# A fused attention and squared-ReLU kernel: values of two groups in one TensorE visit, two half-size visits joined, and a new rule table

## The chip, the core and the metric

The kernel runs on one core of one Trainium2 chip. The metric is the device time of one execution in microseconds (us), lower is better. The core has a matrix engine (TensorE, PE in the profile, with its weight loads listed apart as PEld), VectorE (DVE), ScalarE (ACT), GpSimd (POOL), and SyncE (SP), which here only issues DMAs. Matmuls read SBUF and write PSUM; each engine works off its own instruction list in a fixed order and waits on semaphores for the others.

## What is computed

Two stages run one behind the other, over B = 4 batches of N = 12480 rows of C = 128 columns:

```
h   = mab(I, x)                  # 32 inducing rows attend to all 12480 rows of the batch
y   = mab(x, h)                  # every row of the batch attends to the 32 rows of h
mab(q, kv) = softmax(q @ kv.T / sqrt(128)) @ kv
out = (s * relu(y @ w_in)**2 + b) @ w_out       # d_ff = 2048
```

All data are float32. The first attention needs the whole batch before its softmax is known; the second attention and the two matrix products need only a block of rows and h.

## The kernel before

**Tiling.** A batch is cut into 26 blocks of 480 rows, so there are 104 blocks. For a block the products of the second stage are done in 8 *pairs* of 128 columns of d_ff, 832 pairs in all. A pair (function `pair`) is 8 matmuls of 128x128 weights and 480 columns: two form h (line 1002); `square` and `pair` take the ReLU's square apart into a rounded part and a remainder, and six matmuls into the output bank x (line 1112) take the rounded part with w_lo and w_hi and the remainder with w_hi. The remainder is made by one of three ways: a product on DVE and a subtraction on POOL (line 1056 on POOL, "way P"), both on DVE ("way D"), or a product on DVE and an accumulating DMA that POOL issues (line 1032, "way M").

**Front work.** Beside the pairs of a block runs one *front chain* (`front_work`) in the PSUM bank that the block's output doesn't use. It belongs to attention: for the next batch the scores against the inducing rows (`scores`, 7 groups: six of four blocks and one of two), their maximum (`top`), the values (`values`, 7 groups), the normalisation (`points`) and the small weight product (`w_tiles`); for this batch the second attention (`attend`, also six groups of four blocks and one of two). A block's output matmuls may not start before the front chain of the block ahead is done. The tables ATTEND_AT, SCORES_AT, VALUES_AT and so on say at which block of the batch each unit runs; loads are issued on SP two blocks earlier (AHEAD).

A scores or attention visit of TensorE is up to four matmuls of 128x32 weights and 480 columns, each into its own strip of 32 PSUM partitions. A values visit is 15 matmuls of 128x32 weights (the transposed exponentials, tile eT, three buffers) and 128 columns, which go round the four strips and accumulate; after each visit DVE adds the PSUM sums to the tile accb (line 813). The rows of x for it come in two tiles called xn, of which there are two buffers, so one group's tiles fill both.

**Order.** The program is not ordered by hand: `Plan.run` walks a model of the engines and picks the next instruction by urgency. The numbers of a `Rules` row are the urgencies and leanings it uses (which engine takes a ReLU, when way P, D or M is taken). OPENING holds for the first 16 pairs; then each row of STEADY holds for 32 pairs, four blocks.

Of the kernel before, what the change touches and what calls it, by code (L numbers as in the profile page):

```python
# [10 lines left out]
F32 = mybir.dt.float32  # L11
# [8 lines left out]
P = 128  # L20
# [65 lines left out]
class Rules:  # L86
# [15 lines left out]
    Rules(0.0201, 0.001, -0.4875, 0.022, -8.4567, 5.0037, 2.0571, -1.4711, -15.4208, 3.0931, 2.7863, -1.9358, 2.4132, 1, 0),  # L102
    Rules(0.0217, 0.001, -0.4875, 0.022, -8.4567, 5.0037, 2.0571, -1.4711, -15.4208, 3.0931, 2.0666, -1.9358, 2.4132, 1, 0),
    Rules(0.0167, 0.0365, -0.4924, -0.0196, -12.8895, 5.57, 3.612, -1.5635, -15.4208, 2.9768, 3.1193, 0.5521, 2.3739, 1, 0),
    Rules(0.015, 0.0134, -0.7399, -0.0848, -9.5023, 6.316, 2.0571, -1.5635, -17.0341, 3.1304, 2.2195, -1.3212, 2.9975, 1, 0),
    Rules(0.015, 0.0107, -0.8152, 0.022, -14.1641, 4.9158, -1.107, -0.559, -16.2261, 2.1922, 1.2773, -1.8274, 2.0319, 1, 0),
    Rules(0.0201, 0.0096, -0.624, -0.0242, -8.7384, 5.5129, 2.0571, -1.5635, -15.4208, 2.8109, 2.047, -1.5184, 2.5131, 1, 1),
    Rules(0.0163, 0.001, -1.0478, 0.0978, -8.4567, 8.7374, 2.6103, -1.6884, -17.2651, 3.9096, 3.0379, -2.4315, 2.8881, 1, 0),
    Rules(0.0166, 0.001, -0.624, -0.1167, -5.3436, 5.4916, 3.1805, -0.7229, -17.4773, 2.8109, 2.7209, -1.9358, 2.4761, 1, 0),
    Rules(0.0169, 0.0945, -0.5274, -0.0581, -9.2351, 5.0037, 2.6517, -1.5635, -15.4208, 3.8819, 2.6915, -1.145, 3.3157, 1, 0),  # L110
    Rules(0.015, 0.001, -0.4331, -0.0012, -11.1416, 1.583, -1.107, -0.682, -19.3219, 2.1922, 2.4768, -1.9358, 2.4367, 1, 0),
    Rules(0.0147, 0.001, -0.7361, 0.0372, -5.5428, 6.1406, -1.107, -1.2971, -16.2261, 2.1922, 2.6919, -2.4036, 1.9805, 1, 0),
    Rules(0.0133, 0.001, -0.7846, 0.0725, -10.853, 5.7978, -0.2013, -1.2971, -15.8209, 2.1922, 2.4641, -2.4036, 2.2634, 1, 0),
    Rules(0.0166, 0.084, -0.7108, 0.095, -5.3877, 5.0037, 2.7203, -1.5635, -15.8029, 1.6703, 2.6102, -2.1339, 2.3802, 1, 0),
    Rules(0.0166, 0.084, -0.624, -0.0484, -4.5286, 4.6079, 2.8543, -1.4194, -16.3935, 2.2965, 2.7381, -2.0738, 2.7526, 1, 1),
    Rules(0.0151, 0.084, -0.5751, 0.0036, -9.5767, 5.0037, 2.6127, -1.1092, -15.4208, 2.8842, 3.0781, -0.352, 3.2141, 1, 0),
    Rules(0.0151, 0.084, -0.5751, 0.0036, -9.5767, 5.0037, 2.6127, -1.1092, -15.4208, 2.8842, 3.0781, -0.352, 3.2141, 1, 0),
    Rules(0.0166, 0.084, -0.624, -0.0581, -9.3974, 5.588, 1.858, -1.5635, -15.4208, 3.8843, 1.1082, -0.9457, 2.9743, 1, 0),
    Rules(0.0188, 0.0593, -0.6897, -0.0335, -8.4567, 5.588, 2.6127, -1.9229, -13.1823, 2.6468, 2.5331, -2.1339, 1.9527, 1, 0),
    Rules(0.0199, 0.0017, -0.4795, -0.0514, -9.4081, 6.0969, 2.1224, -1.5635, -17.1933, 2.6161, 2.3942, -1.0923, 2.078, 1, 0),  # L120
# [126 lines left out]
def tile_attn_relu2(ctx: ExitStack, tc: tile.TileContext, xT, xN, xF, indT, w_in, w_out, s_rep, b_rep, outT):  # L247
# [132 lines left out]
    def load_early(j):  # L380
# [7 lines left out]
        plan.events["x", 0, j, 1] = landing(1.2)  # L388

    def load_xn(gate, b, g, half):  # L390
        n, free = ring_in_order("xn", 2)
        yield "SP", 0.05, *free, *gate
        rows = M * blocks_in(g)
        t = xn_pool.tile([P, TH, P], F32, name="xn")
# [934 lines left out]
```

## Time and profile before

| | |
|---|---|
| median of 3 runs | 1519.55 us (1518.22 to 1521.71) |
| the profiled execution | 1518.01 us, of which the span from first to last instruction is 1516.2 us |
| TensorE clock granted | 0.999 of full |
| matmul busy | 1495.3 us, 99% of the span |
| weight loads busy | 1294.9 us, 85% |
| DVE, ACT, POOL busy | 1435.3 us (95%), 1465.4 us (97%), 1443.7 us (95%) |

All engines are busy nearly all the time. A busy share is an average over stages. Matmul records overlap (a record of 0.37 us is followed by the next start 0.20 us later), so the price of a matmul is read from start to start.

### The profile page before, as it was taken

The numbers are of one execution on the slowest core, as the hardware profiler recorded it, in microseconds if no ns is written. First come the engines' busy times: TensorE is split into PE (matmuls) and PEld (weight loads), VectorE is DVE, ScalarE is ACT, GpSimd is POOL, SyncE is SP. The second block draws the span as 40 slices with busy tenths as digits, with TensorE's granted clock in tenths as the row PEclk, the third lists the DMA queues.
The fourth block names the chain that finished last, engine by engine and source line by source line (L and its number), as shares of the span: only waits on it lengthen the run. The fifth ranks groups of instructions, "written<-read, shape, count | busy, mean of one in ns | idle before, by whom it ended". The sixth has DMA issues, their size and how long they took to land.

```text
span 1516.2 us, 25236 instructions
## 1 busy us (share of the span) xinstructions
PE 1495.3 (99%) x8215; PEld 1294.9 (85%) x8215; DVE 1435.3 (95%) x1587; ACT 1465.4 (97%) x1767; POOL 1443.7 (95%) x725
## 2 busy tenths in 40 slices
PE   7899999999999999999999999999999999999998
PEld 5588888888888888888898888888889888888887
DVE  5899999999999999999999999999999999999998
ACT  6899999999999999999999999999999999999997
POOL 2599999999999999999999999999999999999998
PEclk9999999999999999999999999999999999999999
DMA  9244545534454454453455534544533334234332
GB/s 342 65 124 128 140 104 158 143 76 125 104 150 127 114 149 105 135 142 83 127 133 137 144 104 118 163 112 105 120 102 93 79 91 112 56 85 108 91 72 53
DMA packets 73810, 178.91 MB, mean 118 GB/s; under 512 B 13520, under 2 KB 40144, under 8 KB 73680
## 3 DMA queue, kind: packets, MB, share of 16 engines
q1 hardware_dynamic: 59280, 128.51, 27.2%
q0 software_dynamic: 14256, 48.67, 17.3%
q8 instruction: 67, 1.10, 0.3%
q14 instruction: 63, 0.52, 0.1%
q10 hardware_dynamic: 144, 0.12, 0.0%
HBM read 74.56 MB, written 25.56 MB: 66 GB/s over the span
## 4 chain that ended last, share of the span: by engine, by line
PE 69%; ACT 4%; issue 3%; POOL 3%; DVE 2%; DVEq 0%; ACTq 0%; POOLq 0%
PE x L1112 48%; PE h L1002 17%; POOL g L1056 3%; ACT r L1014 2%; ACT g L1080 2%; PE x L853 1%; DVE g L1045 1%; PE x L802 1%; PE x L762 1%; DVE h L1045 0%; DVE r L1016 0%; DVE gm L1027 0%; PE x L717 0%; ACT ob L1125 0%; POOL hm L1032 0%
## 5 line engine op out<-in xcount | busy, mean ns | idle before, releaser
L1056 POOL TENSOR_TENSOR g<-g,g 128x960 fp32r<-128x960 f32 x611 | 1399.2, 2665 | 21.7 <-DVE g L1045 13.4
L1112 PE MATMUL x<-g,w_hi 128*128 128x480 f32 x2932 | 920.1, 367 | 1.5 <-POOL g L1056 1.0
L1080 ACT ACTIVATE g<-r 128x960 fp32r<-128x960 f32 x733 | 713.4, 1008 | 12.0 <-PE x L1112 0.9
L1045 DVE SCALAR_TENSOR_TENSOR g<-h,r 128x960 f32<-128x960 f32 x611 | 688.5, 1146 | 24.2 <-ACT r L1014 13.7
L1014 ACT ACTIVATE r<-h 128x960 f32<-128x960 f32 x648 | 608.6, 970 | 12.5 <-PE h L1002 10.2
L1112 PEld LDWEIGHTS x<-g,w_hi 128*128 128x128 f32 x2932 | 550.8, 189 | 52.5 <-issue 6.3
L1112 PE MATMUL x<-g,w_lo 128*128 128x480 f32 x1466 | 537.4, 367 | 1.4 <-ACT g L1080 1.1
L1002 PE MATMUL h<-a2t,wst 128*128 128x480 f32 x1664 | 485.4, 374 | 3.7 <-DVE g L1045 3.2
L1002 PEld LDWEIGHTS h<-a2t,wst 128*128 128x128 f32 x1664 | 299.2, 189 | 82.2 <-issue 33.1
L1112 PEld LDWEIGHTS x<-g,w_lo 128*128 128x128 f32 x1466 | 277.0, 189 | 24.5 <-issue 2.6
L1016 DVE TENSOR_SCALAR r<-h 128x960 f32<-128x960 f32 x184 | 210.8, 1148 | 5.0 <-PE h L1002 3.8
L1056 DVE TENSOR_TENSOR g<-h,g 128x960 fp32r<-128x960 f32 x122 | 140.7, 1153 | 7.8 <-ACT g L1080 1.2
L1045 DVE SCALAR_TENSOR_TENSOR h<-h,r 128x960 f32<-128x960 f32 x122 | 141.0, 1155 | 0.9 <-ACT r L1014 0.8
L1027 DVE SCALAR_TENSOR_TENSOR gm<-h,r 128x960 f32<-128x960 f32 x99 | 113.3, 1145 | 4.3 <-ACT r L1014 4.1
L1032 POOL DMA_DIRECT2D hm<-gm x99 | 113.7, 1148 | 0.1
L1080 ACT ACTIVATE hm<-r 128x960 fp32r<-128x960 f32 x99 | 99.7, 1007 | 0.7
L1112 PE MATMUL x<-hm,w_lo 128*128 128x480 f32 x198 | 72.8, 368 | 0.0
L1112 PE MATMUL x<-hm,w_hi 128*128 128x480 f32 x198 | 72.5, 366 | 0.0
L1125 ACT ACTIVATE ob<-x,bias 128x480 f32<-128x480 f32 x101 | 66.8, 661 | 1.1 <-PE x L1112 0.5
L1112 PE MATMUL x<-hm,w_neg 128*128 128x480 f32 x198 | 56.3, 366 | 0.0
L1112 PEld LDWEIGHTS x<-hm,w_lo 128*128 128x128 f32 x198 | 37.4, 189 | 3.5 <-DVE hl L891 0.8
L1112 PEld LDWEIGHTS x<-hm,w_neg 128*128 128x128 f32 x198 | 37.4, 189 | 2.7
(152 smaller groups left out, 559.4 us busy)
## 6 DMA issues: line engine op xcount, KB each, us to landing
hm<-gm POOLq DMA_DIRECT2D x99, 480.0 KB, 5.3
xt<-in_xT_dram SPq DMA_DIRECT2D x96, 480.0 KB, 5.2
a2t<-hl SPq DMA_DIRECT2D x412, 60.0 KB, 2.0
out_dram<-ob SPq DMA_DIRECT2D x103, 240.0 KB, 2.1
xn<-in_xN_dram SPq DMA_DIRECT2D x18, 512.0 KB, 4.3
xn<-in_xN_dram SPq DMA_DIRECT2D x18, 448.0 KB, 4.8
wst<-whl SPq DMA_DIRECT2D x48, 64.0 KB, 2.0
g<-in_w_in_dram SPq DMA_DIRECT2D x4, 512.0 KB, 10.3
```

The lines of the kernel that those rows point to most:

```text
L762: nc.tensor.matmul(ps[M * q:M * (q + 1), 0:BLK], ind_sb, xt[:, q % SB], start=True, stop=True)
L802: nc.tensor.matmul(ps[M * c:M * (c + 1), 0:P], eT[0:rows, n], xn_tiles[b, g, half][0][0:rows, n - half * TH], start=n < P // M, stop=n + P ...
L1002: nc.tensor.matmul(h[:, u, 0:BLK], wst[:, n * P:(n + 1) * P], by_turns(A), start=True, stop=True)
L1014: nc.scalar.activation(out=r, in_=hv, func=AF.Relu)
L1016: nc.vector.tensor_scalar(out=r, in0=hv, scalar1=0.0, scalar2=None, op0=ALU.max)
L1027: nc.vector.scalar_tensor_tensor(out=gm, in0=hv, scalar=-1.0, in1=r, op0=ALU.mult, op1=ALU.mult)
L1032: nc.gpsimd.dma_start(out=hi["t"].bitcast(F32).rearrange("p u t -> p (u t)"), in_=gm.rearrange("p u t -> p (u t)"), accum_op=ALU.add,)
L1045: nc.vector.scalar_tensor_tensor(out=g, in0=hv, scalar=0.0, in1=r, op0=ALU.max, op1=ALU.mult)
L1056: eng.tensor_tensor(out=g2, in0=g, in1=hi["t"].bitcast(F32), op=ALU.subtract)
L1080: nc.scalar.activation(out=hi["t"], in_=r, func=AF.Square)
L1112: nc.tensor.matmul(o, w, by_turns(g), start=first and n == 0, stop=left == 0 and n == len(ops) - 1)
L1125: nc.scalar.activation(out=ob, in_=o, func=AF.Identity, bias=bias, scale=1.0)
```

## The change

Three things are done.

1. `values` takes a tuple of groups. Groups (0,1), (2,3) and (4,5) share one visit of 30 matmuls that accumulate in one go, and one addition by DVE behind it; group 6 stays alone. Seven visits a batch become four. The exponentials are transposed in place in s, and the tile eT goes. The second half of a group's rows gets a tile of its own size, xm, so that two groups' rows fit (two buffers of xn and two of xm).
2. The two-block group of the second attention moves from the end of the batch to blocks 8 and 9 (ATTEND gives start and length of each group), so it runs at block 6, in the upper 64 partitions. In batches 0 to 2 the two-block group of the next batch's scores runs in the same visit, in the lower 64 partitions.
3. The places of the units are shifted to suit, and most rows of STEADY have new numbers. OPENING and the first row of STEADY stay.

The diff, cut to its core:

```diff
-ATTEND_AT = (2, 6, 10, 14, 18, 22)
-SCORES_AT = (0, 1, 3, 4, 5, 7, 8)
+ATTEND = ((0, 4), (4, 4), (8, 2), (10, 4), (14, 4), (18, 4), (22, 4))
+ATTEND_AT = (2, 6, 8, 12, 16, 20)
+SCORES_AT = (0, 1, 3, 4, 5, 7, 6)
 TOP_AT = 9
-VALUES_AT = (9, 11, 12, 13, 15, 16, 17)
-H_AT = 19
-W_AT = 20
+VALUES_AT = {(0, 1): 10, (2, 3): 13, (4, 5): 15, (6,): 17}
+H_AT = 18
+W_AT = 19
...
-    Rules(0.0201, 0.001, -0.4875, 0.022, -8.4567, 5.0037, 2.0571, -1.4711, -15.4208, 3.0931, 2.7863, -1.9358, 2.4132, 1, 0),
+    Rules(0.0201, 0.001, -0.4807, 0.022, -8.4567, 4.4152, 2.0571, -1.6802, -15.4208, 3.0931, 2.102, -0.6337, 1.9104, 1, 0),
...
     def load_xn(gate, b, g, half):
-        n, free = ring_in_order("xn", 2)
+        name = ("xn", "xm")[half]
+        n, free = ring_in_order(name, 2)
...
-    def values(b, g, ps, *waits):
+    def values(b, gs, ps, *waits):
         d = st[b]
...
+        for n, g in enumerate(gs):
+            rows = M * blocks_in(g)
+            e = d["s"][0:rows, g]
+            yield "ACT", 0.59, ("top", b), *(waits if n == 0 else ())
+            nc.scalar.activation(
+                out=e, in_=e, func=AF.Exp, bias=d["nm"][0:rows], scale=scale, accum_out=d["l"][0:rows, g:g + 1]
+            )
+            yield "DVE", 0.595
+            nc.vector.transpose(out=e, in_=e)
...
+        for g in gs:
...
+                nc.tensor.matmul(
+                    ps[M * c:M * (c + 1), 0:P], e[:, n], xn_tiles[b, g, half][0][0:rows, n - half * TH],
+                    start=g == gs[0] and n < P // M, stop=g == gs[-1] and n + P // M >= TB,
+                )
...
-    def attend(b, g, ps, *waits):
-        nb = blocks_in(g)
+    def attend(b, g, ps, *waits, also=()):
+        at, nb = ATTEND[g]
+        top = P - M * nb
...
+        other = also and scores(*also, lambda: bank_now, beside=True)
+        more = [next(other)] if also else []
...
+        if also:
+            yield next(other)
+            for want in other:
+                yield want
-        s = ps[0:rows, 0:BLK]
+        s = ps[top:P, 0:BLK]
```

**TensorE, batch 1, the two half-size visits** (x_86 is the bank of the front chain; xt are rows of x, ind_sb the inducing rows, hT the rows of h). Before, the scores visit at block 8 and, 14 blocks on, the attention visit at block 22:

```order
L1002 MATMUL h<-a2t,wst 128x480 x2
L762 MATMUL x_86<-xt,ind_sb 32x480 x2
L1112 MATMUL x_85<-g_6122,w_hi 128x480 x2
...
L1002 MATMUL h<-a2t,wst 128x480 x2
L853 MATMUL x_86<-xt,hT 32x480 x2
L1112 MATMUL x_85<-g_8357,w_lo 128x480
```

Now, at block 6:

```order
L1128 MATMUL x_85<-hm,w_hi 128x480
L1018 MATMUL h<-a2t,wst 128x480 x2
L1128 MATMUL x_85<-g_5794,w_hi 128x480 x2
L863 MATMUL x_86<-xt,hT 32x480 x2
L764 MATMUL x_86<-xt,ind_sb 32x480 x2
L1128 MATMUL x_85<-g_5768,w_lo 128x480
```

The two matmuls of the attention and the two of the scores now stand back to back, where each stood alone among the pairs.

**TensorE, batch 1, the values of the next batch.** Before, one group a visit (two of the seven visits):

```order
L1002 MATMUL h<-a2t,wst 128x480 x2
L802 MATMUL x_85<-xn,eT 32x128 x15
L1002 MATMUL h<-a2t,wst 128x480 x2
...
L1002 MATMUL h<-a2t,wst 128x480 x2
L802 MATMUL x_86<-xn,eT 32x128 x15
L1002 MATMUL h<-a2t,wst 128x480 x2
```

Now, two groups a visit:

```order
L1018 MATMUL h<-a2t,wst 128x480 x2
L806 MATMUL x_85<-xn,s 32x128 x8
L806 MATMUL x_85<-xm,s 32x128 x7
L806 MATMUL x_85<-xn,s 32x128 x8
L806 MATMUL x_85<-xm,s 32x128 x7
L1128 MATMUL x_86<-g_6983,w_hi 128x480 x2
```

All 30 matmuls of a couple of groups follow each other; the matmuls of the pairs that stood between two visits now stand ahead of it or behind it.

**DVE, the same place.** Before, a transpose into eT and an addition for each group:

```order
L797 STREAM_TRANSPOSE eT<-s 128x480
L1045 SCALAR_TENSOR_TENSOR g<-h,r 128x960 x2
L813 TENSOR_TENSOR accb<-x_85,accb 128x128
L1045 SCALAR_TENSOR_TENSOR g<-h,r 128x960
```

Now two transposes in place, with a product of a pair between them, and one step on accb (for the first couple of groups a copy):

```order
L797 STREAM_TRANSPOSE s<-s 128x480
L1061 SCALAR_TENSOR_TENSOR g<-h,r 128x960
L797 STREAM_TRANSPOSE s<-s 128x480
L1061 SCALAR_TENSOR_TENSOR g<-h,r 128x960
L1032 TENSOR_SCALAR r<-h 128x960
L1061 SCALAR_TENSOR_TENSOR g<-h,r 128x960
L814 COPY accb<-x_86 128x128
```

The additions fall from 18 to 9 in the program, the transposes stay at 21.

The two programs have the same matmuls. Counted in DVE's and ACT's order, 208 pairs to a batch, the pairs are shared out like this (before / after):

| batch | way P | way D | way M | ReLU on DVE | ReLU on ACT |
|---|---|---|---|---|---|
| 0 | 156 / 155 | 28 / 29 | 24 / 24 | 44 / 43 | 165 / 166 |
| 1 | 152 / 150 | 31 / 33 | 25 / 25 | 46 / 45 | 163 / 164 |
| 2 | 155 / 156 | 28 / 28 | 25 / 24 | 46 / 48 | 161 / 160 |
| 3 | 148 / 150 | 35 / 34 | 25 / 24 | 48 / 50 | 159 / 156 |
| all | 611 / 611 | 122 / 124 | 99 / 97 | 184 / 186 | 648 / 646 |

The biased copy of the finished block to SBUF (tile ob) runs on ACT 101 / 103 times and on DVE 2 / 0 times.

## Rows read from the trace of the kernel before

**Rows 1.** The page, part 1: busy us, share of the span, instructions, by engine

```profile
PE 1495.3 (99%) x8215; PEld 1294.9 (85%) x8215; DVE 1435.3 (95%) x1587; ACT 1465.4 (97%) x1767; POOL 1443.7 (95%) x725
```

**Rows 2.** Busy us by stretch: from:to, length, PE, PEld, DVE, ACT, POOL, clock, DMA share

```profile
53.00:430.00 377.00, 373.34 (x2038) 322.73 (x2035) 362.98 (x404) 370.69 (x442) 368.17 (x183) 1.00 0.47 122
430.00:796.00 366.00, 365.81 (x2001) 318.93 (x2001) 351.36 (x385) 357.72 (x425) 356.96 (x179) 1.00 0.48 126
796.00:1161.00 365.00, 364.85 (x1999) 319.29 (x1999) 351.49 (x383) 357.92 (x426) 360.61 (x181) 1.00 0.46 119
1161.00:1511.00 350.00, 347.34 (x1691) 305.69 (x1689) 338.64 (x342) 341.45 (x398) 346.92 (x173) 1.00 0.35 86
```

**Rows 3.** PE in order of time (start us, us, instructions): pairs, a four-block visit

```profile
102.13 0.57 PE L1002 MATMUL h<-a2t,wst 128*128 128x480 f32 x2
...
106.18 0.57 PE L1002 MATMUL h<-a2t,wst 128*128 128x480 f32 x2
106.68 1.01 PE L762 MATMUL x<-xt,ind_sb 128*32 128x480 f32 x8
107.62 0.67 PE L1002 MATMUL h<-a2t,wst 128*128 128x480 f32 x2
```

**Rows 4.** PE in order of time: the two-block scores visit of batch 1

```profile
543.77 0.57 PE L1002 MATMUL h<-a2t,wst 128*128 128x480 f32 x2
544.27 1.00 PE L762 MATMUL x<-xt,ind_sb 128*32 128x480 f32 x4
545.20 0.67 PE L1112 MATMUL x<-g,w_hi 128*128 128x480 f32 x2
```

**Rows 5.** PE in order of time: the two-block attention visit of batch 1

```profile
741.12 0.57 PE L1002 MATMUL h<-a2t,wst 128*128 128x480 f32 x2
741.62 1.00 PE L853 MATMUL x<-xt,hT 128*32 128x480 f32 x4
742.55 0.47 PE L1112 MATMUL x<-g,w_lo 128*128 128x480 f32 x1
```

**Rows 6.** PE in order of time: a values visit of batch 1

```profile
563.61 0.57 PE L1002 MATMUL h<-a2t,wst 128*128 128x480 f32 x2
564.11 1.07 PE L802 MATMUL x<-xn,eT 128*32 128x128 f32 x30
565.12 0.67 PE L1112 MATMUL x<-g,w_hi 128*128 128x480 f32 x2
```

**Rows 7.** Line 802: records, duration ns least/median/most, first and last start

```profile
L802 PE MATMUL x<-xn,eT x630: 269/273/297, 198.3 to 1041.5; 128*32 128x128 f32 x135, 64*32 64x128 f32 x23
```

**Rows 8.** Groups by line (busy us, mean ns, idle before): the addition behind a visit

```profile
L813 DVE TENSOR_TENSOR accb<-x,accb 128x128 f32<-128x128 f32 x18 | 5.0, 277 | 0.0
```

**Rows 9.** Who waited for whom, 433 to 796 us: us in total, times, longest

```profile
PEld h L1002 <- issue: 8.8, 19, 0.8
POOL g L1056 <- DVE g L1045: 7.0, 7, 2.4
...
PEld h L1002 <- DVE g L1045: 2.9, 8, 0.8
...
PEld x L802 <- DVE eT L797: 0.9, 3, 0.3
...
PEld x L1112 <- POOL g L1056: 0.3, 2, 0.2
```

**Rows 10.** Who waited for whom, 1161 to 1511 us (the last batch)

```profile
PEld x L1112 <- POOL g L1056: 4.5, 11, 1.0
...
PEld h L1002 <- DVE g L1045: 3.9, 9, 0.8
...
PE x L1112 <- POOL g L1056: 1.0, 2, 0.7
```

**Rows 11.** POOL in order of time: products and the issue of one DMA, last batch

```profile
1299.37 26.90 POOL L1056 TENSOR_TENSOR g<-g,g 128x960 fp32r<-128x960 f32 x12
1326.13 0.98 POOL L1032 DMA_DIRECT2D hm<-gm  x1
1326.73 4.84 POOL L1056 TENSOR_TENSOR g<-g,g 128x960 fp32r<-128x960 f32 x2
```

More of the change, by code (lines that the diff above doesn't have):

```diff
@@ L400, in load_xn @@
         )
-        xn_tiles[b, g, half] = t, ("xn", n)
+        xn_tiles[b, g, half] = t, (name, n)
         plan.events["xn", b, g, half] = landing(1.46)
@@ L737, in w_spread, with scores @@
         plan.events["wst", b, c] = landing(0.7)
-    def scores(b, g, ps, *waits):
+    def scores(b, g, ps, *waits, beside=False):
         nb = blocks_in(g)
@@ L756, in scores @@
                 nc.vector.memset(d["l"][last:P, NG - 1:NG], 0.0)
-        yield "PE", 0.34 + 0.2 * nb, *[("x", b, (GR * g + q) // SB, 1) for q in range(0, nb, SB)], *waits
+        yield "PE", 1.14, *[("x", b, (GR * g + q) // SB, 1) for q in range(0, nb, SB)], *waits
         d = st[b]
@@ L813, in values @@
             nc.vector.tensor_tensor(out=d["acc"], in0=ps[:, 0:P], in1=d["acc"], op=ALU.add)
-        plan.set(("p1", b, g))
+        for g in gs:
+            plan.set(("p1", b, g))
     def points(b, ps, *waits):
@@ L862, in attend @@
         yield "DVE", 0.565
-        mx = sm.tile([P, TB], F32, name="mx2")[0:rows]
+        mx = sm.tile([P, TB], F32, name="mx2")[top:P]
         nc.vector.reduce_max(out=mx, in_=v, axis=AX.X)
@@ L876, in attend @@
         yield "DVE", t3
-        l = sm.tile([P, TB], F32, name="l2")[0:rows]
+        l = sm.tile([P, TB], F32, name="l2")[top:P]
         nc.vector.reciprocal(out=l, in_=sums)
@@ L888, in attend @@
         plan.set(("hl", "got", n))
-        copy(hl[0:rows, 0], s)
+        copy(hl[top:P, 0], s)
         yield "DVE", 0.575
-        nc.vector.tensor_tensor(out=hl[0:rows, 1], in0=s, in1=hl[0:rows, 0].bitcast(F32), op=ALU.subtract)
+        nc.vector.tensor_tensor(out=hl[top:P, 1], in0=s, in1=hl[top:P, 0].bitcast(F32), op=ALU.subtract)
         plan.set(("hl", b, g))
-        halves[b, g] = hl, n, [q for q in range(nb) if (b, GR * g + q) != (0, 0)]
+        halves[b, g] = hl, n, [q for q in range(nb) if (b, at + q) != (0, 0)]
         for q in list(halves[b, g][2]):
@@ L954, in spread @@
         hl, n, left = halves[b, g]
+        at, nb = ATTEND[g]
+        row = P - M * (nb - q)
         for r in range(P // M):
             nc.sync.dma_start(
[L957 removed]
+                out=t[M * r:M * (r + 1)].bitcast(F32), in_=hl[row:row + M, r % 2].bitcast(F32)
             )
@@ L961, in spread @@
             plan.set(("hl", n))
-        a2t[b, GR * g + q] = t, turn
-        plan.events["a2t", b, GR * g + q] = landing(0.7)
+        a2t[b, at + q] = t, turn
+        plan.events["a2t", b, at + q] = landing(0.7)
     def place(k):
@@ L1144, in chain @@
             first = True
-            for f, args in units:
-                for want in f(*args, ps):
+            for f, args, more in units:
+                for want in f(*args, ps, **more):
                     yield (*want, ("ob", blk_g - 1), ("front", blk_g - 1)) if first and blk_g else want
@@ L1164, in tile_attn_relu2 @@
         at = b * NBLK
-        units = [(ATTEND_AT[g - 1], attend, b, g) for g in range(1, NG)]
+        units = [(ATTEND_AT[g - 1], attend, b, g) for g in range(1, len(ATTEND))]
         if b + 1 < B:
             units += [(SCORES_AT[g], scores, b + 1, g) for g in range(NG)]
-            units += [(VALUES_AT[g], values, b + 1, g) for g in range(NG)]
+            units += [(n, values, b + 1, gs) for gs, n in VALUES_AT.items()]
             units += [(TOP_AT, top, b + 1), (H_AT, points, b + 1), (NEXT_AT, attend, b + 1, 0)]
```

112 lines of the change are left out of this document (53 added, 59 removed).

## Prediction, made before the changed kernel ran

> **What bounds the kernel now.** I read the shares of the engines first. All four compute engines are busy for 95 to 99% of the span [rows 1], so shares alone don't name the bound. The stretches do better: between 430 and 796 us, about the second batch, PE is busy for 365.81 of 366 us, while DVE, ACT and POOL have 14.6, 8.3 and 9.0 us left [rows 2]. The order of time says whether this busy PE is at its pace: from 102.13 to 106.18 us twenty matmuls of pairs start, 0.2025 us each, with no gap [rows 3]. A batch has 208 pairs of 8 matmuls, 337.0 us at that pace. The front visits come on top: scores and attention some 1.035 us each, values 1.105 us (below), 7 of each a batch, 22.2 us. Of the 366 us, 6.8 are left for the small front units and for gaps. So in batches 0 to 2 the end is set by the number of PE's starts. The waits agree: in the second batch the largest one that PE's loads charge to another engine is 2.9 us on DVE, in 8 pieces [rows 9].
>
> The last batch differs. No next batch is left to prepare; PE needs 337.0 + 7.2 (seven attention visits) = 344.2 us, and 1161 to 1511 us is 350. PE's loads and matmuls wait there for POOL for 4.5 + 1.0 us and for DVE for 3.9 us [rows 10], and POOL is busy for 346.92 of 350 us [rows 2]. There POOL and PE end nearly together.
>
> **The two half-size visits.** A four-block visit moves the next pair from 106.18 + 0.405 (its two h matmuls) to 107.62: it costs 1.035 us [rows 3]. A two-block scores visit costs 545.20 - 543.77 - 0.405 = 1.025 us [rows 4], a two-block attention visit 742.55 - 741.12 - 0.405 = 1.025 us [rows 5]. So half the blocks cost the same: the strips run side by side, and the price is the entry, one stream of 480 columns and the exit. Joined, the two should cost what a four-block visit costs: 2 x 1.025 - 1.035 = 1.015 us saved, in three batches 3.05 us. Not shown is a visit with two kinds of weights. If the two halves didn't overlap, the second would add its own stream, 545.20 - 544.27 = 0.93 us [rows 4], and 0.1 us would be saved each time, 0.3 in all; more than the whole second visit, 1.025, can't be saved. I take 1.015, because the four-block visit is the nearest row and its strips also hold separate weights. In the last batch the two-block attention stays alone and saves nothing.
>
> The move itself: the attention of blocks 8 and 9 still runs two blocks ahead of its use, like the other groups, and joined visits load two tiles of x, as a four-block visit does. At block 6 the scores' maximum (one DVE step) now goes ahead of the long attention chain on DVE. A block lasts about 14 us (366/26), so I cost that at nothing; without that cover it would be one DVE step a batch.
>
> **Values two by two.** A values visit costs 565.12 - 563.61 - 0.405 = 1.105 us [rows 6]. Its 15 matmuls leave 30 records; the last starts 1.07 - 0.273 = 0.80 us after the first [rows 6, 7], 0.057 us a matmul. Another 15 in the same visit add 0.855 us, so a couple costs 1.96 instead of 2.21: 0.25 us saved, nine times, 2.26 us. What could eat it is the longer row of steps: the visit now waits for two exponentials and two transposes, and PE's list is fixed, so pairs behind it wait too. Before, PE's loads waited for the transposed tile three times in the second batch, 0.3 us each [rows 9]. If each of the nine joined visits waits 0.3 us, the 2.26 becomes -0.4; if the share stays, nothing changes. I take that, since the planner puts the visit later by the length of the chain.
>
> DVE loses 9 additions of 0.277 us [rows 8], 2.5 us, all off PE's path in batches 0 to 2: worth nothing on its own. The loads: four tiles of x rows are now issued on SP in one go where two were, and the copies of the spread attention (a2t) and the outputs queue behind them. They are needed about a block later, some 14 us, so this too is nothing as long as that cover holds. The freed eT ring removes a wait that nobody showed.
>
> **The sum.** 3.05 + 2.26 = 5.3 us of PE time, all before the last batch. On the profiled execution's own 1518.01 us that gives 1512.7; the median of the runs is 1.5 us above it, 1519.55, and gives **1514.2 us**.
>
> **The new rules.** They are the part without a price in the trace. They can only move gaps. On the good side they could take away what PE waits for POOL's products in the last batch: 4.5 us [rows 10]. On the bad side stands the way the work is shared: in the last batch way P goes from 148 to 150 and way M from 25 to 24. A product takes POOL 26.90/12 = 2.24 us, a DMA's issue 0.60 us [rows 11]: 2 x 2.24 - 0.60 = +3.9 us, for an engine with 3.1 us left there [rows 2]. Between -4.5 and +3.9 I take zero, since over the whole program the numbers of ways P, D and M move by two or less.
>
> **Rivals.**
>
> *The last batch lengthens on POOL.* If POOL can't use its 3.1 us of gaps, the 3.9 us go to the end: -5.3 + 3.9 = -1.4, 1518.1 us. For it: POOL is busy for 99% of that stretch and PE waits for it most often there. Against: its work isn't cut at the batch's border, and batch 1 gives POOL two products less.
>
> *The new rules gain more.* -5.3 - 4.5: 1509.7 us. For it: only the last batch has such waits, and its rows of numbers all changed. Against: POOL has more to do there.
>
> *PE isn't the bound, ScalarE is.* ACT is busy for 97% of the span [rows 1], and the change takes two ReLUs off it and gives it two copies, next to nothing. If ACT sets the pace, PE's 5.3 us only turn into gaps, and the time stays at about 1519.2. Against: ACT has 8.3 us left in the second batch and PE 0.2 [rows 2].
> The Trainium skill's page Perfetto Trace Analysis, section Identifying the Most-Contended Engine, says that matmul busy time is a poor measure for TensorE, that its headroom is to be judged by the busy share of the weight loads (and by the FLOPs it does), and that for the other engines occupancy will do. By that rule the 85% of PEld would leave TensorE headroom and put ScalarE first. The trace doesn't bear it out here: the starts of rows 3 follow each other without a gap.
>
> *Slower: batches 0 to 2 become like the last one.* PE gets 5.3/3 = 1.8 us shorter a batch and the other three keep their work. In the third batch POOL would need 156 x 2.24 + 24 x 0.60 = 363.8 us of about 365 - 1.8 = 363.2. From the point where POOL's need passes PE's, PE waits as in the last batch: 4.5 + 1.0 + 3.9 - (0.3 + 2.9) = 6.2 us more a batch [rows 9, 10]. In one batch this only cancels the gain (+0.9); in two it gives -5.3 + 12.4 = +7.1, 1526.7 us. For it: POOL's idle time in the third batch is 4.4 us [rows 2]. Against: POOL runs ahead and behind across batches, and over the whole stretch 53 to 1511 it has 25 us left [rows 2], 5 of which would go.
>
> **How the numbers follow.** The forecast gets 0.55, the rules that gain more 0.13, the last batch on POOL 0.14, ScalarE as the bound 0.08, the slower case 0.10. A measurement of this kernel can tell about 0.2%, 3 us, from no change: under 1516.5 us is faster, over 1522.6 slower. The forecast and the gaining rules lie below, 0.68; POOL in the last batch and ScalarE lie between, 0.22; the last lies above, 0.10. The range goes from the gaining rules, 1509.5, to no gain at all, 1519.5; it leaves out the slower case and the half of the best case that does better still.
>
> **What would show it.** Right: between the ends of the first attention visits of batch 1 and of batch 2 the profile is about 1.8 us shorter; the joined visit of hT and ind_sb moves the next pair by about 1.03 us and the values of two groups by about 1.96 us; the steps of pairs stay at 0.2025 us; PE's share stays at 99% and its waits keep their size. Wrong: a joined visit near 1.95 us (halves that don't overlap); weight loads of pairs that wait for POOL in batches 0 to 2 as in rows 10; a last batch that is longer than before by 2 us or more; waits ahead of the values visits of 0.3 us and more each.

## The result: slower by 0.6%

Before 1518.22 us (1517.27 to 1521.71, 5 runs), after 1528.38 us (1526.08 to 1529.34, 5 runs): ratio 1.0061, 95% interval 1.0046 to 1.0076. The forecast was 1514.2, with a range of 1509.5 to 1519.5. The profiled execution of after took 1529.34 us, with a span of 1527.6.

The page of after, part 1, as [rows 1]:

```profile
PE 1496.8 (98%) x8215; PEld 1296.0 (85%) x8215; DVE 1439.3 (94%) x1580; ACT 1469.3 (96%) x1767; POOL 1442.5 (94%) x723
```

Nothing here explains the 11.4 us by which the span grew: all engines do the same work in a longer span. The stretches are cut at the first pairs of the batches, as in [rows 2]:

```profile
53.00:428.00 375.00, 370.47 (x2024) 322.13 (x2024) 359.69 (x396) 368.20 (x438) 362.33 (x180) 1.00 0.47 122
428.00:798.00 370.00, 367.15 (x1999) 318.46 (x1998) 354.03 (x385) 360.17 (x428) 354.27 (x177) 1.00 0.47 123
798.00:1167.00 369.00, 365.72 (x2004) 319.35 (x2003) 352.82 (x384) 359.80 (x426) 365.14 (x181) 1.00 0.46 117
1167.00:1521.00 354.00, 349.48 (x1699) 307.98 (x1697) 341.75 (x343) 343.59 (x398) 349.73 (x174) 1.00 0.35 84
```

From the first output matmul of a batch to that of the next (batch 0 from its first h matmul, batch 3 up to the last output matmul), the four batches took 374.8, 365.3, 365.4 and 352.1 us before and 375.1, 370.5, 368.4 and 354.4 after. In batches 0 to 2, where both savings apply and where I expected 1.8 us less each, the time grew by 0.3, 5.2 and 3.0 us.

**The savings are there.** The joined visit of batch 1, PE in order of time:

```profile
515.84 0.57 PE L1128 MATMUL x<-g,w_hi 128*128 128x480 f32 x2
516.34 0.60 PE L863 MATMUL x<-xt,hT 128*32 128x480 f32 x2
516.35 0.60 PE L764 MATMUL x<-xt,ind_sb 128*32 128x480 f32 x2
516.76 0.57 PE L863 MATMUL x<-xt,hT 128*32 128x480 f32 x2
516.77 0.57 PE L764 MATMUL x<-xt,ind_sb 128*32 128x480 f32 x2
517.28 0.47 PE L1128 MATMUL x<-g,w_lo 128*128 128x480 f32 x1
```

It moves the next pair by 517.28 - 515.84 - 0.405 = 1.035 us, exactly a four-block visit [rows 3]: the strips of hT and ind_sb start 0.01 us apart. A values visit of two groups, first and last rows:

```profile
652.48 0.37 PE L1128 MATMUL x<-g,w_hi 128*128 128x480 f32 x1
652.78 0.65 PE L806 MATMUL x<-xn,s 128*32 128x128 f32 x16
...
654.05 0.68 PE L806 MATMUL x<-xm,s 128*32 128x128 f32 x13
654.66 0.67 PE L1018 MATMUL h<-a2t,wst 128*128 128x480 f32 x2
```

That is 654.66 - 652.48 - 0.2025 = 1.98 us, where 1.96 was forecast. Summed over the program, from start to start, the steps into, within and out of front visits fell from 97.9 to 89.6 us; twelve of these steps became plain steps of pairs (2.4 us), so PE's work fell by 5.9 us; 5.3 was the forecast. (Small waits inside the front visits are counted in these steps.)

**What ate them.** Subtract 0.2025 us from every step between two matmuls of pairs, and PE's gaps are left. They were 29.3 us before (10.0, 4.5, 4.4 and 10.3 by batch) and are 43.0 after (11.0, 9.7, 9.2, 13.0), and another 3.0 us are steps at half clock: +16.7 - 5.9 = +10.8, against a span that grew by 11.4. Of the 3.0, 1.6 stand behind the largest gap (below); 1.4 stand in the opening, at 57 to 60 us, in place of a wait of 1.2 us that the profile of before has there, and cost next to nothing. Who was waited for, 53 to 1521 us, rows of PE and its loads (us in total, times, longest):

```profile
PEld h L1018 <- DVE g L1061: 18.5, 34, 2.6
...
PEld x L1128 <- POOL g L1072: 9.4, 26, 0.8
...
PEld x L1128 <- DMA hm<-gm: 2.3, 3, 1.2
...
PE h L1018 <- DMA a2t<-hl: 3.0, 2, 2.4
```

Two of them are new: no row of before charges PE to a DMA of a2t or of hm. The first two in the same view of before, 53 to 1511 us:

```profile
PEld h L1002 <- DVE g L1045: 15.5, 32, 2.6
...
PEld x L1112 <- POOL g L1056: 5.6, 14, 1.0
```

The a2t row shows only part of what late copies cost. At 168 and 848 us PE stands still for 1.9 us each; the view puts these waits down to DVE, but the last copy of the tile landed 0.24 us ahead of the matmul that ends them, and both gaps are gone in the runs below in which no copy is late. The largest gap of the program, batch 1:

```profile
528.35 0.66 DVE L905 TENSOR_TENSOR hl<-x,hl 64x480 fp32r<-64x480 f32 x1
529.74 7.26 SPq L972 DMA_DIRECT2D a2t<-hl  x8
530.67 0.87 POOL L1048 DMA_DIRECT2D hm<-gm  x1
531.93 0.57 PE L1018 MATMUL h<-a2t,wst 128*128 128x480 f32 x2
537.30 0.64 PE L1018 MATMUL h<-a2t,wst 128*128 128x480 f32 x2 [2.37 <-DMA a2t<-hl]
538.65 0.61 PE L1128 MATMUL x<-g,w_hi 128*128 128x480 f32 x1
539.05 0.61 PE L1128 MATMUL x<-g,w_lo 128*128 128x480 f32 x1
```

The joined visit's attention is spread into a2t for blocks 8 and 9. DVE ends the last step of its chain (hl) at 529.01, 12.7 us after the visit. SP issues the output of the block ahead at 529.35 and only then the copies, from 529.74 on; POOL issues the accumulating DMA of a way-M pair 0.9 us later; the four copies of block 8 have landed at 537.16, and its first pair, due at about 534.9, starts at 537.30. The rows behind it are 0.40 us apart instead of 0.20, and the stretch view shows the clock (column behind POOL's):

```profile
531.00:534.00 3.00, 3.00 (x19) 2.80 (x16) 2.94 (x5) 2.91 (x5) 3.00 (x3) 1.00 0.85 164
537.30:541.00 3.70, 3.70 (x11) 3.22 (x12) 1.16 (x1) 1.97 (x2) 3.03 (x2) 0.61 0.07 18
```

Behind a gap of 2.4 us PE ran at half of full speed, 1.2 GHz, for eight steps: 1.6 us more. Before, at the same block:

```profile
516.00 1.01 PE L853 MATMUL x<-xt,hT 128*32 128x480 f32 x8
...
524.53 5.32 SPq L956 DMA_DIRECT2D a2t<-hl  x8
524.88 0.64 DVE L891 TENSOR_TENSOR hl<-x,hl 128x480 fp32r<-128x480 f32 x1
```

Here hl ends 9.5 us after the visit; SP is free, and its first copy (of the half that is ready earlier) goes out 1.0 us ahead of that; block 8's four copies had landed at 528.75, and its first pair read them at 531.55: 2.8 us to spare. From the visits on, the first copy went from 8.5 to 13.4 us, issue to landing from 4.2 to 7.4, and the need from 15.55 to 18.56: 2.8 - 4.9 - 3.2 + 3.0 = -2.3, within 0.1 us the wait of 2.37 shown. Of the 4.9, 3.2 are the chain on DVE, the rest is SP's list, on which the output now stands ahead.

### The profile page after: what moved, and what is told of

Its sections match the earlier page's. It is cut to its first block, busy times and chain, and to the rows that moved or that the text cites. A ratio compares the mean times of both kernels' runs of the same rounds, so it can differ in the third digit from the quotient of the medians.

```text
span 1527.6 us, 25178 instructions
## 1 busy us (share of the span) xinstructions
PE 1496.8 (98%) x8215; PEld 1296.0 (85%) x8215; DVE 1439.3 (94%) x1580; ACT 1469.3 (96%) x1767; POOL 1442.5 (94%) x723
## 5 line engine op out<-in xcount | busy, mean ns | idle before, releaser
L1061 DVE SCALAR_TENSOR_TENSOR g<-h,r 128x960 f32<-128x960 f32 x611 | 688.7, 1146 | 23.5 <-ACT r L1030 13.4
L1018 PEld LDWEIGHTS h<-a2t,wst 128*128 128x128 f32 x1664 | 300.1, 189 | 88.1 <-issue 36.9
L1048 POOL DMA_DIRECT2D hm<-gm x97 | 109.0, 1123 | 0.9 <-PE x L1128 0.7
```

The costliest lines, as they stand in the source:

```text
L1018: nc.tensor.matmul(h[:, u, 0:BLK], wst[:, n * P:(n + 1) * P], by_turns(A), start=True, stop=True)
L1048: nc.gpsimd.dma_start(out=hi["t"].bitcast(F32).rearrange("p u t -> p (u t)"), in_=gm.rearrange("p u t -> p (u t)"), accum_op=ALU.add,)
L1061: nc.vector.scalar_tensor_tensor(out=g, in0=hv, scalar=0.0, in1=r, op0=ALU.max, op1=ALU.mult)
```

## Experiments

### Which part of the change costs?

Three theories: the joined visit delays block 8 (T1); the new rules are at fault (T2); any order that the rules weren't fitted to loses time (T3). First, values two by two alone: the changed kernel with the half-size visits apart, the old rules and the old places (each couple of groups stands where its later group stood).

```diff
-ATTEND = ((0, 4), (4, 4), (8, 2), (10, 4), (14, 4), (18, 4), (22, 4))
-ATTEND_AT = (2, 6, 8, 12, 16, 20)
-SCORES_AT = (0, 1, 3, 4, 5, 7, 6)
+ATTEND = ((0, 4), (4, 4), (8, 4), (12, 4), (16, 4), (20, 4), (24, 2))
+ATTEND_AT = (2, 6, 10, 14, 18, 22)
+SCORES_AT = (0, 1, 3, 4, 5, 7, 8)
...
-VALUES_AT = {(0, 1): 10, (2, 3): 13, (4, 5): 15, (6,): 17}
-H_AT = 18
-W_AT = 19
+VALUES_AT = {(0, 1): 11, (2, 3): 13, (4, 5): 16, (6,): 17}
+H_AT = 19
+W_AT = 20
...
-    Rules(0.0201, 0.001, -0.4807, 0.022, -8.4567, 4.4152, 2.0571, -1.6802, -15.4208, 3.0931, 2.102, -0.6337, 1.9104, 1, 0),
+    Rules(0.0201, 0.001, -0.4875, 0.022, -8.4567, 5.0037, 2.0571, -1.4711, -15.4208, 3.0931, 2.7863, -1.9358, 2.4132, 1, 0),
...
```

> One part alone: values two by two in one visit (tile eT gone, xm added), half-size visits apart as before, the old rules. Theories: (T1) the time comes from the joined half-size visit at block 6, whose attention rows reach block 8 late; (T2) it comes from the new rule rows; (T3) it comes from the order as such: the old order had been fitted by trials, and any other order loses some 5 to 10 us, whatever its edit. T1 and T2: the 2.3 us of PE time show, 1516 us against 1518 (ratio 0.998 to 1.000), and the first rows of every group of four blocks reach PE 2 us or more ahead of use. T3: 1522 us or more.

Measured: 1533.4 us, ratio to before 1.0097 (1.0082 to 1.0112).

Second, the joined visit alone, with one group a values visit and the old rules:

```diff
-VALUES_AT = {(0, 1): 10, (2, 3): 13, (4, 5): 15, (6,): 17}
+VALUES_AT = {(0,): 9, (1,): 10, (2,): 11, (3,): 13, (4,): 14, (5,): 15, (6,): 17}
```

and the rows of STEADY as in the first.

> One part alone: the half-size attention moved to blocks 8 and 9 and joined with the half-size scores, values one group a visit, the old rules. T1: 3 us of PE time gained, but PE waits for the rows of block 8 in block 7 of batches 0 to 2, 2 us and more each, so 1522 to 1527 us. T2: no such waits, 1515 us. T3: 1522 us or more, with the added waits spread over all batches and not at block 7.

Measured: 1534.87 us, 1.0110 (1.0095 to 1.0125).

Third, the whole change without its rules (its one edit is that exchange of rows in STEADY), and fourth the converse, the kernel before with the new rows of STEADY and nothing else:

> The changed kernel with the old rule rows: structure alone. T1: waits at block 7 stay, 1522 to 1528 us. T2: they go, 1512 to 1514 us, as forecast for the PE time. T3: 1520 to 1530 us, waits anywhere.

> The kernel before with the new rule rows: rules alone. T1: no change, 1516 to 1520 us. T2: 1524 to 1530 us, most of the loss of the changed kernel and of its 5 us of PE time besides. T3: 1522 us or more, since this order wasn't fitted either.

Measured: 1541.4 us, 1.0155 (1.0140 to 1.0170), and 1534.45 us, 1.0107 (1.0090 to 1.0124).

All four are slower than both kernels. Each half of the change takes work from PE and costs 15 to 16 us with the old rules; the new rules cost 16 us where they weren't fitted, and take 13.0 off (1541.4 to 1528.4) where they were. So neither the joined visit nor the rules by themselves are the cause: T3. The expectations that went with T1 and T2 missed, and T3 set the loss too low: it said 5 to 10 us, and 1520 to 1530 us for the third run, which took 1541.4.

### How far does a mere change of order go?

The kernel before, with each number of its rules moved by about 2% at random; nothing else:

```diff
-    Rules(0.0201, 0.001, -0.4875, 0.022, -8.4567, 5.0037, 2.0571, -1.4711, -15.4208, 3.0931, 2.7863, -1.9358, 2.4132, 1, 0),
+    Rules(0.0201, 0.001, -0.4927, 0.0221, -8.8608, 5.024, 2.0511, -1.5074, -15.4821, 3.1493, 2.7659, -1.9442, 2.4626, 1, 0),
...
```

> The kernel before with every number of its STEADY rows moved by some 2% at random (same structure, same number of instructions). (T3) an order that wasn't picked by trials loses 8 to 16 us: 1526 to 1535 us. If the old order were nothing special: 1517 to 1521 us.

Measured: 1525.21 us, 1.0043 (1.0028 to 1.0058): 5.6 us, just under the range that T3 gave, but clearly a loss with no work added (one random draw; others were not tried). Its gaps are 36.9 us instead of 29.3, and the row that grew is PE's wait for an h bank that DVE still reads:

```profile
PEld h L1002 <- DVE g L1045: 18.7, 34, 2.6
...
PE h L1002 <- DVE g L1045: 6.8, 7, 2.3
```

### Is it the late transfers?

Two theories for the gaps of after: DMAs that land late, with the clock that falls behind them (D), or gaps between the compute engines (G). In the changed kernel, the order untouched, the h matmuls read w_hi from block 1 on, so nothing on PE waits for a2t:

```diff
+    fake = w_hi.rearrange("p f d -> p (f d)")
...
-            nc.tensor.matmul(h[:, u, 0:BLK], wst[:, n * P:(n + 1) * P], by_turns(A), start=True, stop=True)
+            nc.tensor.matmul(
+                h[:, u, 0:BLK], wst[:, n * P:(n + 1) * P], by_turns(fake[:, 0:BLK] if k >= NPAIR else A), start=True, stop=True
+            )
```

> The changed kernel with its order untouched on every engine; from block 1 on the h matmuls read the resident w_hi instead of the tile a2t that DMAs spread from the attention (the attention's result is left out of the output; the DMAs still run). So no matmul waits for those DMAs. Theories: (D) what the changed order loses against the old one is DMA that lands later than the order allows for (a2t, the accumulation of way M) and the drop of TensorE's clock behind the longest of these waits; (G) it is gaps between the compute engines (h banks that DVE frees late, POOL's products late), and a wait taken away comes back at the next one. D: 1518 to 1521 us, some 8 us under the changed kernel's 1528.4. G: 1525 us or more.

Measured: 1521.29 us (10 runs), 1.0017 (1.0008 to 1.0027).

The same and the accumulated remainder (hm with w_neg) replaced as well:

```diff
-        ops = [(w_neg[:, 2 * i + u, :], hi["t"][:, u, :]) for u in range(2)]
+        ops = [(w_neg[:, 2 * i + u, :], fake[:, 0:BLK] if k >= NPAIR else hi["t"][:, u, :]) for u in range(2)]
```

> As the run without a2t, and the two w_neg matmuls of way M read w_hi too (the accumulated product is left out of the output; its DMA still runs), so that no matmul of a pair waits for a DMA. D: 1516 to 1519 us, 2 us more gained. G: 1525 us or more.

Measured: 1520.59 us (10 runs), 1.0015 (1.0006 to 1.0025). The same two edits in the kernel before, as a control, and in the whole change with the old rules:

> The same two replacements in the kernel before, order untouched. Its trace shows no wait of the pairs for these DMAs, so both theories: 1516.5 to 1518.5 us, no change. A gain of over 3 us would mean that the replacement itself makes matmuls cheaper, and the runs with it could not be read.

> The same two replacements in the changed kernel with the old rules (1541.4 us). D: 1528 to 1533 us: 5.9 us of waits for a2t, 1.3 for way M and 2 us of low clock go, and what is left over the kernel before are gaps that the unfitted rules leave in the order. G: 1538 us or more.

Measured: 1519.03 us, 1.0000 (0.9991 to 1.0010), and 1534.46 us, 1.0101 (1.0085 to 1.0116).

The waits for a2t are worth 7.1 us in after (1528.38 to 1521.29), those for hm 0.7 us more, which is within the noise and not the 2 us expected, and nothing at all in before. With the old rules 6.9 us go, and 1534.46 lies between the ranges of D and G. D holds for these 7 to 8 us. The rest is G: without any such wait after still isn't faster than before, although PE has 5.9 us less to do. Its gaps are then 34.5 us, and the waits between compute engines are as large as they were with the late copies:

```profile
PEld h L1020 <- DVE g L1065: 19.3, 36, 2.6
...
PEld x L1132 <- POOL g L1076: 9.4, 25, 0.9
```

### Why does a2t land late?

Over all a2t tiles, from the first issue to the last landing: where way M's DMA is under way for more than 1.5 us of that time, the median is 6.0 us, elsewhere 4.1 (61 and 42 tiles in after; in before 6.1 and 4.2, 55 and 48 tiles). So either the collision is what counts (C), or the longer chain ahead of the copies alone (L). The changed kernel with way M's DMA cut to 8 of its 960 columns, all issues in their places:

```diff
-                out=hi["t"].bitcast(F32).rearrange("p u t -> p (u t)"),
-                in_=gm.rearrange("p u t -> p (u t)"), accum_op=ALU.add,
+                out=hi["t"].bitcast(F32).rearrange("p u t -> p (u t)")[:, 0:8],
+                in_=gm.rearrange("p u t -> p (u t)")[:, 0:8], accum_op=ALU.add,
```

> The changed kernel, order untouched, with the accumulating DMA of way M cut from 960 to 8 columns a partition (the rest of the accumulation is left out, so the output lacks it). In the changed kernel the four late a2t tiles (block 8 of batches 0 and 1, block 4 of batch 2, block 18 of batch 3) were issued within 1 us of such a DMA and took 6.2 to 7.4 us from first issue to landing, where tiles that meet none take 4.1. Theories: (C) the collision makes them late: they land 4.1 us after first issue, the waits of 0.8 to 2.5 us at these four places go, way M's own waits go too, 1518 to 1521 us as without any wait for DMAs. (L) the attention chain is late by itself and its four DMAs are slow to issue: the waits stay within a microsecond, 1526 us or more.

Measured: 1520.47 us (10 runs), 1.0006 (0.9996 to 1.0015): 7.9 us less than after, so C: without the collision the tiles are in time. The DMA issues of after, then of this run (instructions, KB each, median us to landing):

```profile
hm<-gm POOLq DMA_DIRECT2D x97, 480.0 KB, 5.7
...
a2t<-hl SPq DMA_DIRECT2D x412, 60.0 KB, 2.6
```

```profile
hm<-gm POOLq DMA_DIRECT2D x97, 4.0 KB, 3.0
...
a2t<-hl SPq DMA_DIRECT2D x412, 60.0 KB, 2.0
```

And the place of the largest gap in this run:

```profile
527.27 0.66 DVE L905 TENSOR_TENSOR hl<-x,hl 64x480 fp32r<-64x480 f32 x1
528.65 5.79 SPq L972 DMA_DIRECT2D a2t<-hl  x8
529.59 0.87 POOL L1048 DMA_DIRECT2D hm<-gm  x1
...
533.71 0.65 PE L1018 MATMUL h<-a2t,wst 128*128 128x480 f32 x2
534.19 0.37 PE L1128 MATMUL x<-g,w_lo 128*128 128x480 f32 x1
534.39 0.37 PE L1128 MATMUL x<-g,w_hi 128*128 128x480 f32 x1
```

The chain is as long and the issue as late as in after, but the four copies have landed 4.9 us after the first issue instead of 7.4; block 8 starts on time, with 0.14 us to spare, and the granted clock behind it stays at 1.00. So the longer chain has used up the margin of 2.8 us, and the collision adds the rest. In after, four tiles landed late (block 8 of batches 0 and 1, block 4 of batch 2, block 18 of batch 3); each met a way-M DMA that was issued 0.3 to 0.9 us behind its first copy, and PE's gaps there are 1.9, 2.5, 1.9 and 0.8 us.
The Trainium skill's page DMA: Bandwidth & Descriptors, section Queues, rings and completion order, says that each DMA engine takes turns between the queues that have work for it, a packet at a time. The 2 us that an a2t tile loses beside a way-M DMA (6.0 to 4.1) agree with that; how the turns are taken no run here shows.

### Two attempts to mend it

The scores' maximum goes ahead of the attention's chain on DVE. Planned behind it:

```diff
-        if also:
-            yield next(other)
-            for want in other:
-                yield want
+        late = next(other) if also else None
...
+        if also:
+            yield late
+            for want in other:
+                yield want
```

> The changed kernel with the maximum of the joined scores planned behind the attention chain and not ahead of it. This lets the planner build a new order, so the total may move by some 5 to 15 us for that alone (as the four kernels with old or exchanged rules did). What is to be read is the joined visit: from its first matmul to the end of hl (12.2 to 12.7 us in batches 0 and 1 in the changed kernel, 9.1 to 9.9 us in the kernel before at block 6). (L) the step ahead makes the chain late: 1 us or more is gained there and block 8 waits under 1 us. (C) alone: the chain's length stays within 0.7 us. Time 1525 to 1538 us in either case.

Measured: 1536.76 us, 1.0116 (1.0099 to 1.0133). And the joined visit one block earlier, at block 5:

```diff
-ATTEND_AT = (2, 6, 8, 12, 16, 20)
-SCORES_AT = (0, 1, 3, 4, 5, 7, 6)
+ATTEND_AT = (2, 5, 8, 12, 16, 20)
+SCORES_AT = (0, 1, 3, 4, 6, 7, 5)
```

> The changed kernel with the joined visit at block 5 and scores group 4 at block 6, one block of 14 us more for the attention rows of blocks 8 and 9; a new order again. Whatever makes them late, block 8 then waits for nothing in batches 0 to 2, and up to 6 us are gained on that; against it stands the loss of an order that the rules weren't fitted to, 5 to 15 us. (T3, order) 1528 to 1540 us. If the placing were the main cause: 1520 to 1524 us.

Measured: 1539.42 us, 1.0141 (1.0120 to 1.0163). Both lose 8 to 11 us to after. In the first the chain from the joined visit to the end of hl is shorter by 0.6, 1.4 and 0.4 us in batches 0 to 2 (12.7 to 11.3 in batch 1), so the maximum ahead of it is part of its length, in two batches less than the 1 us expected. At block 8 both did what they were meant to: its tile lands 2.2 to 4.1 us ahead of the need in the one, 14 to 19 us in the other. But other tiles are late now (landed less than 0.4 us ahead of the need), five in the one and three in the other, and the gaps grew from 43.0 to 52.8 and 54.5 us. As times these two are no test of the chain; as orders they show that the late tile isn't bound to the joined visit. The four orders of the first section have two to six late tiles each, the shaken one two; the kernel before has none, its least margin of all being 0.7 us.

### Does a refitted order bring the saving back?

Three kernels whose rules were searched anew, each for its structure, with a planner that counts the a2t copies and way M's sum as landing later. The edit, beside new numbers in STEADY:

```diff
-M_LAND = 8.0
+M_LAND = 9.0
...
-        plan.events["a2t", b, at + q] = landing(0.7)
+        plan.events["a2t", b, at + q] = landing(2.2)
```

First the joined visit at block 5, then at block 6, then the kernel before as the control:

> The changed kernel with the joined visit at block 5, rules searched anew for it, and a planner that counts an a2t tile as landing 1.5 us later and way M's sum 1 us later. Two theories. S: the new structure pays as soon as its order is fitted; then there are no late a2t tiles, PE's gaps are near the 29 us of the kernel before, and the time is 1512 to 1514 us (1518.5 less 5.9, plus at most a microsecond or so). F: rules found off the chip don't fit its engines, whatever the structure; gaps are 36 to 46 us as in the shaken and the changed kernel, and the time is 1518 to 1528 us. Under both no a2t tile should come late, if the collision with way M's transfer is what made it late.

> The changed kernel itself (joined visit at block 6) with rules searched anew and the same later landings in the planner. S: 1512 to 1514 us, gaps near 29 us. F: 1518 to 1528 us, gaps 36 to 46 us. If the late tiles at block 8 alone were the loss, it is at 1520 to 1521 as without waits for a2t, and the 7 to 8 us are back.

> The kernel before with rules searched anew in the same way and the same later landings: the control for the other two. S: its gaps stay near 29 us and it is at 1517 to 1520 us, 4 to 6 us above the other two. F: the new order fits the chip less well than the old one; 1522 to 1530 us. Under either, the difference between this run and the other two is what the structure is worth when both are fitted by the same means: 4 to 6 us if PE's saved work comes back, 0 if the gaps take it.

Measured: 1523.8 us, 1.0032 (1.0021 to 1.0044); 1526.07 us, 1.0047 (1.0033 to 1.0060); 1523.85 us, 1.0035 (1.0022 to 1.0048). The late tiles are gone: at most one each, with 0.2 us of gap or less. But with rules found by the same means, the new structure is level with the old one or 2.2 us behind: its gaps are 39.8 and 40.9 us, those of the control 32.8, so 7 to 8 us of gaps take the place of the work that PE was saved. S, that the structure pays once its order is fitted, is out. F, that rules found off the chip fit no structure well, gave the times rightly, yet doesn't say why the structure is worth nothing. None of the three beats the kernel before.

### Who takes the saving?

Two theories: PE and the other three engines bound the kernel together (B), or the gaps belong to the changed structure (U). From block 3 on, the product on DVE, the square on ACT and the subtraction behind them cover 432 of 480 columns; PE's output matmuls still read 480 columns (240 of them twice), and their pace stays at 0.2025 us; way M's DMA is cut as above. The order stays:

```diff
+    def twice(x):
+        return x[:, 0:BLK // 2].unsqueeze(2).to_broadcast((P, BLK // 2, 2))
...
+        w = BLK if k < 3 * NPAIR else 432
...
-        nc.vector.scalar_tensor_tensor(out=g, in0=hv, scalar=0.0, in1=r, op0=ALU.max, op1=ALU.mult)
+        nc.vector.scalar_tensor_tensor(out=g[:, :, 0:w], in0=hv[:, :, 0:w], scalar=0.0, in1=r[:, :, 0:w], op0=ALU.max, op1=ALU.mult)
...
-        eng.tensor_tensor(out=g2, in0=g, in1=hi["t"].bitcast(F32), op=ALU.subtract)
+        eng.tensor_tensor(out=g2[:, :, 0:w], in0=g[:, :, 0:w], in1=hi["t"].bitcast(F32)[:, :, 0:w], op=ALU.subtract)
...
-        nc.scalar.activation(out=hi["t"], in_=r, func=AF.Square)
+        nc.scalar.activation(out=hi["t"][:, :, 0:w], in_=r[:, :, 0:w], func=AF.Square)
...
-            nc.tensor.matmul(o, w, by_turns(g), start=first and n == 0, stop=left == 0 and n == len(ops) - 1)
+            nc.tensor.matmul(o, w, twice(g) if k >= 3 * NPAIR else by_turns(g), start=first and n == 0, stop=left == 0 and n == len(ops) - 1)
```

> The changed kernel in its own order with way M's transfer cut to 8 columns (1520.5 us as such), and from block 3 on 432 instead of 480 columns in the product on DVE, the square on ACT and the subtraction on POOL or DVE, so these three engines have some 5 to 10% less to do in those lines; the output matmuls read 480 columns as before (240 of them twice). Two theories. B: PE and the other three bound the kernel together, and the 5.9 us that PE was saved are gaps in which it waits for the others; then, with the others lighter, this kernel is 5 to 6 us faster than the next one. U: the gaps belong to the changed structure itself (longer chains, tighter places), whatever the others have to do; then the two are within 2 us of each other. Both kernels should lose most of their gaps: 1490 to 1510 us.

> The same cuts in the kernel before. B: 5 to 6 us slower than the changed kernel with them. U: within 2 us of it.

> The first of these with the squares on ACT at their full 480 columns, DVE's products and POOL's subtractions at 432. If ScalarE sets the pace (the rival of the prediction), this run is near 1520 us; if it is DVE and POOL, near the first of these runs, within 3 us.

Measured: 1501.12 us for the changed kernel (1499.58 to 1503.68, 0.9890, 0.9877 to 0.9904), 1505.13 for the kernel before (1503.56 to 1507.46, 0.9916, 0.9903 to 0.9930), 1508.45 with ACT's squares in full (0.9934, 0.9920 to 0.9948). Part 1 of the page, the changed kernel and the kernel before:

```profile
PE 1480.7 (99%) x8215; PEld 1307.0 (87%) x8215; DVE 1359.7 (91%) x1580; ACT 1416.8 (94%) x1767; POOL 1328.4 (89%) x723
```

```profile
PE 1485.4 (99%) x8215; PEld 1307.7 (87%) x8215; DVE 1355.0 (90%) x1587; ACT 1413.2 (94%) x1767; POOL 1330.5 (89%) x725
```

With the others lighter the changed kernel is 4.0 us faster than the kernel before, where with full work it was level (1520.5 to 1519.6). Gaps fell from 35.9 to 18.4 us in the one and from 29.3 to 16.0 in the other. The two waits that had grown in after are among those that shrink in the changed kernel (53 to 1500 us):

```profile
PEld h L1023 <- DVE g L1066: 10.1, 19, 2.6
...
PEld x L1134 <- POOL g L1077: 0.8, 1, 0.8
```

So B: most of PE's saved time had turned into waiting for engines that had no less to do. The difference is 4.0 and not 5 to 6. With four runs each it is known to about 3 us, so the times alone don't exclude the 2 us of U; the gaps speak for B, since the changed kernel's excess of gaps fell from 6.6 to 2.4 us. These 2.4 us may belong to the structure. The kernel before has no run with full work and way M's DMA cut; that this DMA delays nothing there is taken from its run without waits for DMAs (1519.03).

By batch, as above, in the profiled executions (one each):

| | batch 0 | batch 1 | batch 2 | batch 3 |
|---|---|---|---|---|
| before | 374.8 | 365.3 | 365.4 | 352.1 |
| after with way M's DMA cut | 373.0 | 366.1 | 365.3 | 353.8 |
| before, the others lighter | 372.3 | 363.1 | 363.5 | 344.4 |
| after, the others lighter | 370.9 | 361.5 | 361.7 | 346.6 |

With the others lighter each of the batches 0 to 2 is 1.4 to 1.8 us shorter in the changed kernel than in the kernel before, near the 1.8 that was forecast; with full work only batch 0 is, and batches 1 and 2 gain nothing. The last batch, in which PE was saved nothing, is 1.7 to 2.2 us longer in either case. What makes it so is open: its rows of rules and its places are new, and no run takes it alone.

ScalarE isn't the other bound alone: of the 19.4 us from 1520.5 to 1501.1, its squares account for 7.3, DVE and POOL together for 12.0 (6.7 and 10.9 by the ratios to before, which took 1519.62 us beside the first of these runs and 1518.01 beside the other two). The expectation for ACT's squares in full fits neither of its two cases. Which of DVE and POOL counts more was not tested.

## Why the prediction was wrong, point by point

- **What bounds the kernel: wrong where it said "the end is set by the number of PE's starts".** Before had 29.3 us of gaps between pairs, 4.4 to 10.3 a batch; I read 365.81 busy of 366 us [rows 2] as a PE without gaps, but overlapping records hide small ones. PE is bound together with other engines, whose work the change leaves alone. The saving is real and is paid out when they are lighter (4.0 us), not when they are full (0.9 us slower without late copies; after the same refit level with the joined visit at block 5 and 2.2 us slower with it at block 6). This alone would have made the forecast "same".
- **The half-size visits, 3.05 us, and the values, 2.26 us: right.** 1.035 and 1.98 us a visit were measured, for 1.035 and 1.96 forecast, and 5.9 us less work in all. No waits came up ahead of the values visits: PE's loads waited for the transposed tile for 0.3 us in all, once, where it had been 2.4 us in eight pieces.
- **"I cost that at nothing", of the move: wrong.** The attention of blocks 8 and 9 was said to run "still two blocks ahead of its use, like the other groups". But the margin isn't two blocks, some 28 us: behind the chain on DVE, the copies and their landing 2.8 us were left at this place. The chain grew by 3.2 us, SP's list by 1.7, the landing by 3.2 beside way M's DMA, and the need came only 3.0 later. The four late tiles, with the clock behind them, are 7 to 8 us. Two of them are the joined visit's. Of the other two, block 4 of batch 2 stands behind a visit that kept its place and belongs to the new order; the visit of block 18 in batch 3 was moved too, from block 14 to 16, where block 18 is the first of its four blocks.
- **"Nothing as long as that cover holds", of the loads on SP: right for the loads, wrong for the queue.** No row charges PE to a load of x. But I looked at SP alone for what the copies meet; POOL's queue, which shares the DMA engines, I hadn't put beside it.
- **"Between -4.5 and +3.9 I take zero", of the rules: the sum's other wrong term.** The bounds came from the waits for POOL and the numbers of ways in the last batch, which hardly moved. What the runs show to count is the order itself: 13.0 us on the new structure, 5.6 for a shake of 2%, 15 and more for rules of another structure. A zero stood for a term that is larger than the whole saving.
- **The rivals.** *ScalarE is the bound* had the right mechanism, "PE's 5.3 us only turn into gaps", and with 1519.2 nearly the time without late transfers (1520.5), but named one engine: ScalarE's squares are worth 7.3 us of the 19.4, and DVE and POOL together the rest. *Batches 0 to 2 become like the last one* had the right sign, and its 1526.7 us lie near the 1528.4 by luck; its waits were to be for POOL and DVE, and PE's loads do wait longer for both, 3.8 us for POOL's products (5.6 to 9.4) and 3.0 for DVE's (15.5 to 18.5). The late a2t tiles, the larger part of the loss, stood in no rival.
- **The last batch on POOL:** it is 2.3 us longer, but 0.8 of its gaps are a late a2t tile, and POOL has gaps of 4.3 us there (349.73 of 354). It is still 2.2 us longer when POOL, with DVE and ACT, is lighter, which speaks against POOL's load as the cause.

## What to carry to other kernels

In this kernel, statically ordered and with all engines at 94% or more, work taken from one of them turned into its gaps until the others got lighter too; where several engines are that busy, expect no more until a run says so. A new order has a price of its own: shaking the old one gives a first idea of it (5.6 us here; rules of another structure cost 15 and more). Of each step that is moved, follow the chain to the last landing, and set what other queues send at that time beside the margin. Read PE's gaps from start to start: busy shares of overlapping records hide them.

## What the runs showed of the hardware

- A joined visit whose strips hold two kinds of weights (hT and ind_sb) costs what four strips of one kind cost, 1.035 us; 15 more values matmuls in a visit cost 0.87 us.
- A 60 KB copy from SBUF to SBUF lands in a median of 2.6 us in after and 2.0 with way M's DMA cut. A tile's four copies take 4.1 us in after from the first issue to the last landing, and 6.0 beside an accumulating DMA of 480 KB on POOL's queue. With that DMA cut to 4 KB, 4.0 to 4.1.
- After PE had waited 2.4 us, the granted clock was 0.61 over the next 3.7 us, and eight steps took 0.40 us instead of 0.20. The wait cost 1.6 us more than its own length. Not every such wait does: the clock stayed at 1.00 behind the waits of 1.9 us at 168 and 848 us, and behind one of 2.4 us at 684 us in the run with the maximum planned behind the chain; behind the same wait of 2.3 us for DVE in the opening it fell in the profiled execution of after (57 to 60 us) and stayed in that of before.
